# Issuing conv 2's output stores on GpSimd one group later, behind the next group's accumulating load

## The chip, the cores and the metric

The kernel runs on one core of a Trainium2 chip. The metric is the device time of one execution in microseconds (us); the median of several runs is given. The engines of the core are TensorE (PE, matrix products), VectorE (DVE), ScalarE (ACT), GpSimd (POOL) and SyncE (SP, which here only issues DMAs). Each engine takes its instructions in the order in which they stand in its queue, and waits at an instruction whose inputs aren't ready; all that stands behind it waits too.

## The reference

A residual block: group norm, SiLU and a 3x3 convolution, twice, with a time embedding added between, and the input added at the end. The input `x` is 2 images of 512 channels of 64 x 64, in bfloat16.

```python
B, C, HW, E = 2, 512, 64, 1152
def gn(z, gamma, beta):                 # 4 groups of 128 channels
    zr = z.reshape(B, G, (C // G) * H * W)
    mu = zr.mean(-1).reshape(B, G, 1)
    var = ((zr - mu) ** 2).mean(-1).reshape(B, G, 1)
    zn = ((zr - mu) / jnp.sqrt(var + eps)).reshape(B, C, H, W)
    return zn * gamma.reshape(1, C, 1, 1) + beta.reshape(1, C, 1, 1)
...
h = conv3(_silu(gn(x, g1, be1)), w1)
emb = _silu(t_emb) @ w_emb
h = h + emb.reshape(B, C, 1, 1)
h = conv3(_silu(gn(h, g2, be2)), w2)
return x + h
```

## The kernel before

Both convolutions (`layer` 0 and 1, here conv 1 and conv 2) are done by a fast scheme over rows: four output rows come from six row combinations of the activated input ("positions" 0 to 5), of which 1 and 2 (and in one chunk 3 and 4) are transformed over columns as well ("nested", tiles `nst`). The others take three column taps directly (tiles `mid` for 3 and 4, `acc` for 0 and 5).

A *chunk* is half an image, 32 rows: (b, ch) with b the image and ch the half, so there are four chunks in a convolution. For each chunk, four *groups* follow, one for each tile of 128 output channels (`ot`). A convolution thus has 16 groups, numbered 0 to 15 (`grp`). One group on TensorE is: nested products (L741), `mid` products (L730), `acc` products (L730).

The transformed input of a chunk is a tile V; V of the next chunk is made while the groups of this one run, by a background planner with due times (`bg`, `produce_V`): for each of the four input channel tiles, SP loads `src` (L420), ACT does SiLU into `ak` (L427) and a scaled copy (L433), and DVE adds and subtracts rows and columns (L442 to L491). GpSimd writes border rows with memsets (L414, L416). In conv 2, for the second chunk only, the first of the row adds (L442) is done by DMA instead: `ROWS_BY_DMA` makes GpSimd issue two accumulating DMAs from `ak` to `ak` (L437), a half each. DVE's L448 is the first instruction that needs both halves.

The scale and bias of a group norm come from `gn_scale_bias`. It has two small steps on GpSimd, L179 and L186 (`var`), between DVE steps L178 and L187. For the second image of conv 2 this is called in group 3 (`aux_plan`).

The output of a group is put together in a tile `yst` (`xr` in the last two groups) of the pool `stg`, which has three buffers. ACT copies `nst` and `mid` out (L782, L797); DVE combines rows (L804 to L813) and takes the `acc` banks in (L827). The end of group n, `close_group` and the `fin` that it returns, is carried out within group n+1, between its nested products and their evacuation (`close_prev`). For groups 0 to 13 of conv 2 (`X_BY_DMA`), `fin` adds the residual by DMA: GpSimd issues a load of `x` that accumulates into `yst` (L843), and then the store of `yst` to the output (L844), which needs the load's data. In what follows load n and store n are those of group n. For groups 14 and 15 `x` is loaded into `xr` by SP (L686) and added by DVE (L810, L815), and SP stores the output. These `xr` tiles come from the same three buffers, so the load of `xr` in group 14 waits for store 11, and that in group 15 for store 12.

The order on each engine is the order of the program, as far as the framework's scheduler keeps it; waits between engines and DMAs are placed by the framework.

Of the kernel before, what the change touches and what calls it, by code (L numbers as in the profile page):

```python
# [10 lines left out]
ALU = mybir.AluOpType  # L11
# [51 lines left out]
def kernel(  # L63
# [13 lines left out]
    nc = tc.nc  # L77
# [33 lines left out]
    x_v = x.rearrange("b (ct p) h w -> b ct p (h w)", p=P)  # L111
    out_v = out.rearrange("b (ct p) h w -> b ct p (h w)", p=P)
# [47 lines left out]
    def flat(t):  # L160
        return t[:].rearrange("p r w -> p (r w)")
# [32 lines left out]
    def after(inst, dep):  # L194
        if dep is not None:
            tc.add_manual_dep(inst.ins, dep.ins.name, SYNC_DEP, reason="dma ordering")
        return inst

    def gram_pe(pieces, grf):
# [323 lines left out]
    for i, prm in enumerate((g1, be1, g2, be2)):  # L523
        nc.scalar.dma_start(
            out=gparm[CT * i:CT * (i + 1), :],
            in_=prm.rearrange("(ct p) -> ct p", p=P),
# [70 lines left out]
    st2 = {}  # L597
    pend = []
    deferred = []

    def aux_plan(layer, g):
        acts = []
# [25 lines left out]
    for layer in range(2):  # L628
        for idx, (b, ch) in enumerate(chunks):
            for ot in range(CT):  # L630
# [49 lines left out]
                rows = slice(ch * CR * W, (ch + 1) * CR * W)  # L680
# [3 lines left out]
                if layer == 1 and not by_dma:  # L684
                    xr = stg.tile([P, CR, W], BF16, tag="io")
                    nc.sync.dma_start(  # L686
                        out=xr[:], in_=x_v[b, ot][:, rows].rearrange("p (r w) -> p r w", w=W))
# [7 lines left out]
                yst = xr if layer == 1 and not by_dma else stg.tile([P, CR, W], F16, tag="io", name="yst")  # L695
# [3 lines left out]
                last_two = grp - (len(chunks) * CT - 2) if layer == 1 else -1  # L699
# [74 lines left out]
                def scaled(o, i, f, on_act=ACT_SCALES(layer, grp)):  # L774
                    if on_act:
                        nc.scalar.activation(out=o, in_=i, func=ACT.Copy, scale=f)  # L776
                    else:
                        nc.vector.tensor_scalar(out=o, in0=i, scalar1=f, scalar2=None, op0=ALU.mult)
# [24 lines left out]
                def rows_mid(scaled=scaled, add_x=layer == 1 and not by_dma, y4=y4, sts=sts, msl=msl, tt=tt, qs=qs):  # L803
                    nc.vector.tensor_tensor(out=sts[:, 2:4], in0=msl[:, 0:2], in1=msl[:, 2:4], op=ALU.add)  # L804
                    nc.vector.tensor_tensor(out=sts[:, 0:2], in0=msl[:, 0:2], in1=msl[:, 2:4], op=ALU.subtract)
                    nc.vector.tensor_tensor(out=tt[:, 0], in0=sts[:, 2], in1=sts[:, 3], op=ALU.add)
                    scaled(qs[:, 0], sts[:, 0], 8.0)
                    nc.vector.tensor_tensor(out=tt[:, 1], in0=qs[:, 0], in1=sts[:, 1], op=ALU.add)  # L808
                    if add_x:
                        nc.vector.tensor_tensor(out=tt[:], in0=tt[:], in1=y4[:, 0:4:3], op=ALU.add)  # L810
                    scaled(qs[:, 0], sts[:, 0], 2.0)
                    scaled(qs[:, 1], sts[:, 2], 4.0)
                    nc.vector.tensor_tensor(out=qs[:] if add_x else y4[:, 1:3], in0=sts[:, 1:4:2], in1=qs[:], op=ALU.add)  # L813
                    if add_x:
                        nc.vector.tensor_tensor(out=y4[:, 1:3], in0=qs[:], in1=y4[:, 1:3], op=ALU.add)  # L815

                def close_group(layer=layer, b=b, ch=ch, ot=ot, rows=rows, yst=yst, y4=y4, tt=tt, accs=accs,
                                ssum=ssum, ssq=ssq, on_dve=on_dve, by_dma=by_dma):
                    if not on_dve:
                        for k in range(2):  # L820
                            nc.tensor.matmul(accs[(0, 5)[k]], lhsT=id_end[:, k],
                                             rhs=tt[:, k].rearrange("p t (e w) -> p t e w", e=2), start=False, stop=True)
                    for k in range(2):
                        kw = {"accum_out": ssum[:, ch, k:k + 1]} if layer == 0 else {}
                        acc = accs[(0, 5)[k]].rearrange("p t e w -> p t (e w)")
                        if on_dve:
                            nc.vector.scalar_tensor_tensor(out=y4[:, (0, 3)[k]], in0=acc, scalar=(0.25, 1.0)[k],  # L827
                                                           in1=tt[:, k], op0=ALU.mult, op1=ALU.add, **kw)
                        else:
                            nc.scalar.activation(out=y4[:, (0, 3)[k]], in_=acc, scale=(0.25, 1.0)[k],  # L830
                                                 func=ACT.Identity if layer == 0 else ACT.Copy, **kw)

                    def fin():
                      if layer == 0:
                        yf = flat(yst)
                        nc.sync.dma_start(out=h_scr[b, ot][:, rows], in_=yf)
                        junk = otmp.tile([P, CR * W], F16, tag="sts", name="junk")
                        nc.scalar.activation(out=junk[:, 0:CR * W // 2].rearrange("p (f t w) -> p f t w", f=2, w=W),  # L838
                                             in_=y4[:, 1:3], func=ACT.Identity, accum_out=ssum[:, ch, 2:3])
                        nc.scalar.activation(out=junk[:], in_=yf, func=ACT.Square,  # L840
                                             scale=float(HW) ** -0.5, accum_out=ssq[:, ch:ch + 1])
                      elif by_dma:
                        nc.gpsimd.dma_start(out=flat(yst), in_=x_v[b, ot][:, rows], accum_op=ALU.add)  # L843
                        nc.gpsimd.dma_start(out=out_v[b, ot][:, rows], in_=flat(yst))  # L844
                      else:
                        nc.sync.dma_start(out=out_v[b, ot][:, rows], in_=flat(yst))
                    return fin
# [33 lines left out]
                if first_set:  # L881
                    for pos in DIRECT + NESTED:
                        open_acc(pos)
                    aux = None
                    for ct in range(CT):
                        if ct % 2 == 0:
                            aux = ps_two.tile([P, 2, NFREE], F32, tag="two", name="aux1")
                        gn1_load(ct)
                        gn1_stats(aux[:, ct % 2], ct)
                        for pos in DIRECT + NESTED:  # L890
                            for kx in KX_ORDER:
                                mm_direct(pos, ct, kx, ct == 0 and kx == KX_ORDER[0],
                                          (pos in (1, 2, 3, 4) or on_dve) and ct == CT - 1 and kx == KX_ORDER[-1])
                    evac_mid(0)
                    evac_mid()
                    for _ in range(3):
                        bg.tick()
                    rows_mid()
                    for _ in range(3):
                        bg.tick()  # L900
                    pend.append(close_group)
                else:
                    for pos in NESTED:
                        mms(pos)
                        bg.tick()
                    if layer == 0 and grp == NFLAT - 1:
                        for f in flat_cols:
                            f()
                    if is_flat:
                        close_prev(lambda: evac_mid(0))  # L910
                    elif last_two == 1:
                        evac_nested()
                    else:
                        close_prev(evac_nested)
                    if not is_flat:
                        cols_mid()
                    mms(3)
                    bg.tick()
                    mms(4)
                    bg.tick()  # L920
                    run_aux(layer, grp)
                    if four:
                        evac_nested(1)
                        cols_mid(1)
                    else:
                        evac_mid()
                    rows_mid()
                    if last_two == 0:
                        deferred.append((end_rows, close_group))
                    elif last_two == 1:  # L930
                        ends, close = deferred.pop()
                        ends()
                        close()()
                        close_halves()
                    else:
                        for pos in (0, 5):
                            mms(pos)
                            bg.tick()
                        pend.append(close_group)
# [41 lines left out]
```

## Time and profile before

| | us |
|---|---|
| median of 3 runs | 508.08 |
| the runs | 506.97, 508.08, 510.08 |
| profiled execution | 509.58 |
| its span (first to last instruction) | 507.8 |
| TensorE busy | 486.2 (96% of the span) |
| VectorE busy | 426.1 (84%) |
| ScalarE busy | 350.9 (69%) |
| GpSimd busy | 44.1 (9%) |

The table is of one profiled execution but for its first two rows. Busy times are shares of the span and overlap each other; a wait on an engine counts only if what ends last is held up by it. Conv 2 runs from about 290 us to the end; one of its groups takes about 14 us. Loads 0 to 13 of `x` start between 299.03 and 481.69 us, and the stores between 304.94 and 487.64. A load lands 5.5 us after its issue (median), a store 3.0 us.

### The profile page before, as it was taken

How to read it: one execution, taken by the hardware profiler on the slowest of the kernel's cores; microseconds unless marked ns; L12 is line 12 of the kernel's file. 1: busy time of each engine (PE TensorE's matmuls, PEld its weight loads, DVE VectorE, ACT ScalarE, POOL GpSimd, SP SyncE). 2: the span in 40 equal slices, each digit the busy share in tenths (PEclk: the TensorE clock that was granted, in tenths of full speed). 3: DMA queues.
4: the chain of work that ended last, by engine and by line, in shares of the span. 5: the costliest groups of instructions: out<-in, count | busy, mean ns of one | idle time of the engine just before them, and what ended most of it. 6: DMA issues, size and time to landing. Idle time of an engine off the chain costs nothing. (4 is left out here: it accounts for less than half of the span.)

```text
span 507.8 us, 8116 instructions
## 1 busy us (share of the span) xinstructions
PE 486.2 (96%) x3140; PEld 285.8 (56%) x3140; DVE 426.1 (84%) x946; ACT 350.9 (69%) x341; POOL 44.1 (9%) x92
## 2 busy tenths in 40 slices
PE   4899999899999999999999999989999999999996
PEld 4865454555555555555555555545555555557784
DVE  4789899999986994469999999768998999547776
ACT  4688899699965954478999899509779633333350
POOL 1210000100000000010011002221011101110100
PEclk9679999999999999999999999989999999999999
DMA  8939231142431421133476334735554632325442
GB/s 309 365 110 333 80 119 64 45 158 92 118 95 53 142 74 43 41 121 109 152 199 178 105 87 112 155 84 130 123 134 119 124 74 55 94 71 124 122 87 83
DMA packets 24144, 61.99 MB, mean 122 GB/s; under 512 B 2219, under 2 KB 11563, under 8 KB 23723
## 3 DMA queue, kind: packets, MB, share of 16 engines
q1 hardware_dynamic: 18864, 44.64, 26.6%
q0 software_dynamic: 5184, 16.85, 15.2%
q8 instruction: 24, 0.39, 0.3%
q14 instruction: 13, 0.11, 0.1%
q10 hardware_dynamic: 59, 0.01, 0.0%
HBM read 42.54 MB, written 16.78 MB: 117 GB/s over the span
## 5 line engine op out<-in xcount | busy, mean ns | idle before, releaser
L730 PE MATMUL acc<-V,R 128*128 128x512 f16 x744 | 173.5, 390 | 3.4 <-DVE yst L827 2.6
L730 PE MATMUL mid<-V,U 128*128 128x512 f16 x720 | 167.2, 387 | 1.7 <-ACT rm L797 1.7
L730 PEld LDWEIGHTS <-R 128*128 128x128 bf16 x792 | 77.6, 99 | 95.6 <-issue 5.9
L730 PEld LDWEIGHTS <-U 128*128 128x128 f16 x720 | 70.2, 98 | 88.0 <-issue 5.3
L741 PE MATMUL nst<-V,U 128*128 128x256 f16 x1024 | 116.7, 273 | 0.0
L741 PEld LDWEIGHTS <-U 128*128 128x128 f16 x1056 | 103.3, 98 | 18.6
L782 ACT ACTIVATE rm<-nst 128x1024 f16<-128x1024 f32 x68 | 67.2, 1013 | 37.4 <-PE nst L741 24.7
L427 ACT ACTIVATE ak<-src,nb_all,sc_all 128x2112 f16<-128x2112 f16 (+1 forms) x28 | 59.9, 2143 | 9.3 <-DVE V L475 5.5
L433 ACT ACTIVATE ak<-ak 128x2112 f16<-128x2112 f16 x32 | 62.7, 1959 | 1.1 <-DVE V L473 0.4
L797 ACT ACTIVATE rm<-mid 128x1024 f16<-128x1024 f32 x30 | 30.4, 1015 | 27.3 <-PE mid L730 27.3
L776 ACT ACTIVATE qs<-sts 128x512 f16<-128x512 f16 x36 | 22.0, 626 | 28.8 <-DVE sts L804 22.9
L442 DVE TENSOR_TENSOR ak<-ak 128x2112 f16<-128x2112 f16 x28 | 34.9, 1250 | 5.7 <-ACT ak L433 5.7
L475 DVE TENSOR_TENSOR V<-ak 128x1056 f16<-128x1056 f16 x56 | 39.2, 700 | 0.3
L827 DVE SCALAR_TENSOR_TENSOR yst<-acc,tt 128x512 f16<-128x512 f32 x52 | 35.5, 683 | 1.8 <-PE acc L730 1.3
L789 DVE TENSOR_TENSOR tu<-rm 128x512 f16<-128x512 f16 x34 | 14.3, 419 | 24.8 <-ACT rm L782 24.6
L254 ACT ACTIVATE S<-R 128x1536 f16<-128x1536 bf16 (+1 forms) x28 | 31.4, 1155 | 2.7 <-DVE U L251 1.4
L838 ACT ACTIVATE junk<-yst 128x1024 f16<-128x1024 f16 x16 | 16.9, 1058 | 23.3 <-DVE yst L813 23.2
L840 ACT ACTIVATE junk<-yst 128x2048 f16<-128x2048 f16 x16 | 30.5, 1906 | 1.2 <-DVE yst L827 1.0
L251 DVE TENSOR_TENSOR U<-S 128x1536 f16<-128x1536 f16 x32 | 29.7, 948 | 0.0
L804 DVE TENSOR_TENSOR sts<-rm 128x1024 f16<-128x1024 f16 x32 | 21.9, 685 | 7.3 <-ACT rm L797 7.0
L491 DVE TENSOR_TENSOR V<-V 128x512 f16<-128x512 f16 x64 | 26.1, 431 | 0.0
L448 DVE TENSOR_TENSOR ak<-ak 128x1056 f16<-128x1056 f16 x32 | 22.5, 702 | 3.6 <-DMA ak<-ak 3.4
(124 smaller groups left out, 445.9 us busy)
## 6 DMA issues: line engine op xcount, KB each, us to landing
src<-h_scr SPq DMA_DIRECT2D x16, 528.0 KB, 4.1
h_scr<-yst SPq DMA_DIRECT2D x16, 512.0 KB, 2.7
yst<-in_x_dram POOLq DMA_DIRECT2D x14, 512.0 KB, 5.5
out_dram<-yst POOLq DMA_DIRECT2D x14, 512.0 KB, 3.0
src<-in_x_dram SPq DMA_DIRECT2D x12, 528.0 KB, 7.9
R<-in_w_dram SPq DMA_DIRECT2D x16, 384.0 KB, 4.2
xt<-in_x_dram SPq DMA_DIRECT2D x8, 512.0 KB, 5.9
g1t<-in_w_dram SPq DMA_DIRECT2D x16, 192.0 KB, 5.0
```

The costliest lines, as they stand in the source:

```text
L251: nc.vector.tensor_tensor(out=o, in0=i0, in1=i1, op=op)
L254: ts = lambda o, i, f: nc.scalar.activation(out=o, in_=i, func=ACT.Copy, scale=f)
L427: nc.scalar.activation(out=at[:, lo - r0:hi - r0, 1:W + 1], in_=sap, func=ACT.Silu, bias=nb_all[:, layer, b, ct:ct + 1], scale=sc_all[:, l ...
L433: nc.scalar.activation(out=diff, in_=same, func=ACT.Copy, scale=-4.0)
L442: nc.vector.tensor_tensor(out=diff, in0=diff, in1=below, op=ALU.add)
L475: nc.vector.tensor_tensor(out=pair(k).rearrange("p q (t w) -> p q t w", w=WP), in0=in0, in1=in1, op=op)
L730: nc.tensor.matmul(out, lhsT=w_direct(pos, ct, kx), rhs=rhs, start=first, stop=last)
L741: nc.tensor.matmul(accs["nst", (pos - 1) // 2][bank][:, q, :, plane, :], lhsT=lhsT, rhs=rhs.rearrange("p (t w) -> p t w", w=HALF), start=s ...
L782: nc.scalar.activation(out=raw[:, bank].rearrange("p q t e w -> p (q t e w)"), in_=accs["nst", k][bank][:].rearrange("p q t e w -> p (q t ...
L797: i_a = nc.scalar.activation(out=msl[:, 1 - k:4 - k:2].rearrange("p s t w -> p s (t w)"), in_=accs["mid", k][:].rearrange("p s t e w -> p ...
L827: nc.vector.scalar_tensor_tensor(out=y4[:, (0, 3)[k]], in0=acc, scalar=(0.25, 1.0)[k], in1=tt[:, k], op0=ALU.mult, op1=ALU.add, **kw)
L840: nc.scalar.activation(out=junk[:], in_=yf, func=ACT.Square, scale=float(HW) ** -0.5, accum_out=ssq[:, ch:ch + 1])
```

## The change

`fin` no longer issues the store of its own group. It issues the load, then the store that is still kept from the group before, and keeps its own. The store that is issued gets an edge to the load just issued (`behind`): it is an order for the scheduler alone and adds no wait on a semaphore. In the last two groups (`last_two >= 0`), after the row step, what is still kept is issued at once. Line numbers in the profile of before are those of the old file: L843 and L844 are the two calls with a minus.

```diff
+    ORDER_DEP = mybir.DependencyInfo(mybir.DependencyClass.NoSync, mybir.DependencyReason.SCHED_ONLY)
+
+    def behind(inst, dep):
+        if dep is not None:
+            tc.add_manual_dep(inst.ins, dep.ins.name, ORDER_DEP, reason="order")
+        return inst
...
+    to_store = []
+
+    def store_out(inst):
+        while to_store:
+            dst, y = to_store.pop()
+            behind(nc.gpsimd.dma_start(out=dst, in_=y), inst)
...
                       elif by_dma:
-                        nc.gpsimd.dma_start(out=flat(yst), in_=x_v[b, ot][:, rows], accum_op=ALU.add)
-                        nc.gpsimd.dma_start(out=out_v[b, ot][:, rows], in_=flat(yst))
+                        store_out(nc.gpsimd.dma_start(out=flat(yst), in_=x_v[b, ot][:, rows], accum_op=ALU.add))
+                        to_store.append((out_v[b, ot][:, rows], flat(yst)))
...
                     rows_mid()
+                    if last_two >= 0:
+                        store_out(None)
```

## The prediction

> **What bounds the kernel now.** I read the busy table, then the waits by total, then the order of time on GpSimd (POOL), VectorE (DVE) and TensorE (PE) from 316 to 342 us, the chain that ended last, and TensorE's clock in short stretches.
>
> ```profile
> PE 486.2 (96%) x3140; PEld 285.8 (56%) x3140; DVE 426.1 (84%) x946; ACT 350.9 (69%) x341; POOL 44.1 (9%) x92
> ```
>
> TensorE is the bound. POOL works 44 us of 508, so its own idle time costs nothing: what the change can be worth lies in what stands *behind* a waiting store on POOL's queue, if TensorE in the end waits for that. The waits (waiter, releaser, us in total, times, longest):
>
> ```profile
> POOL out_dram L844 <- DMA yst<-in_x_dram: 70.8, 14, 6.1
> DVE sc_all L187 <- POOL var L186: 6.8, 3, 4.1
> DVE ak L448 <- DMA ak<-ak: 3.4, 1, 3.4
> PE acc L730 <- DVE yst L827: 2.6, 1, 2.6
> PE mid L730 <- ACT rm L797: 1.7, 2, 1.1
> ```
>
> The first row is what the change aims at: 14 stores wait 70.8 us for their own loads. The last two rows are what TensorE loses to other engines in conv 2, 4.3 us. POOL's order of time shows what hangs on the first (start, us, instruction, idle before it and its releaser):
>
> ```profile
> 316.62 0.87 POOL L843 DMA_DIRECT2D yst<-in_x_dram  x1 [7.02 <-DVE ee L229]
> 319.61 0.87 POOL L437 DMA_DIRECT2D ak<-ak  x1 [2.12 <-ACT ak L433]
> 324.32 0.56 POOL L844 DMA_DIRECT2D out_dram<-yst  x1 [3.85 <-DMA yst<-in_x_dram]
> 324.88 0.90 POOL L437 DMA_DIRECT2D ak<-ak  x1
> ...
> 333.34 0.89 POOL L843 DMA_DIRECT2D yst<-in_x_dram  x1 [7.39 <-DVE yst L827]
> 339.15 0.56 POOL L844 DMA_DIRECT2D out_dram<-yst  x1 [4.92 <-DMA yst<-in_x_dram]
> 339.73 0.25 POOL L179 TENSOR_SCALAR var<-var 128x4 f32<-128x4 f32 x1
> ```
>
> Twice a store holds up something wanted. Store 1 (324.32) stands between the two halves of a row add by DMA (L437); store 2 (339.15) stands ahead of the group norm's `var`. Who waits for these, from the orders of time of DVE and PE:
>
> ```profile
> 328.98 0.71 DVE L448 TENSOR_TENSOR ak<-ak 128x1056 f16<-128x1056 f16 x1 [3.45 <-DMA ak<-ak]
> 331.03 0.68 DVE L827 SCALAR_TENSOR_TENSOR yst<-acc,tt 128x512 f16<-128x512 f32 x1
> 341.14 0.16 DVE L187 TENSOR_TENSOR sc_all<-var,gb 128x4 f32<-128x4 f32 x1 [4.08 <-POOL var L186]
> ...
> 331.77 7.13 PE L730 MATMUL acc<-V,R 128*128 128x512 f16 x24 [2.61 <-DVE yst L827]
> 371.43 5.50 PE L730 MATMUL mid<-V,U 128*128 128x512 f16 x24 [0.65 <-ACT rm L797]
> 386.82 5.50 PE L730 MATMUL mid<-V,U 128*128 128x512 f16 x24 [1.06 <-ACT rm L797]
> ```
>
> The first chain is whole: late second half, DVE idle 3.45 us, L827 late, TensorE idle 2.61 us. Its next 24 matmuls take 7.13 us, where the same 24 take 5.50 later on. Two short stretches say why (stretch, length, PE busy, granted clock, DMA share, GB/s):
>
> ```profile
> 328.78:332.19 3.41, 0.80 (x6) 1.00 0.00 0
> 332.19:335.60 3.41, 3.41 (x9) 0.50 0.25 22
> ```
>
> After a stretch in which TensorE worked only 0.80 us, the granted clock was half for 3.41 us: 7.13 - 5.50 = 1.6 us more. From 386.82 on TensorE has no wait left up to its last matmul at 503.8; the chain that ended last is matmuls alone there. So whatever TensorE gains up to 386.82 reaches the end whole, and nothing later can add to it.
>
> **The change part by part.** The order of instructions as built is the same on PE, DVE, ACT and SP. On POOL, store n stands right behind load n+1; stores 12 and 13 close the row. The edge adds no semaphore: store n still waits for load n, which has then landed long before (load 1 by 324.3, store 1 now behind load 2 at 333).
>
> *Second half of the row add.* Load 1, store 0, then both L437 halves, with no wait between the halves: the second goes out at 319.61 + 0.89 = 320.50 instead of 324.88, 4.4 us earlier. But it must be moved too, and store 0 now lies ahead of both halves. DMA work, as share times length, from quiet stretches: one load 3.60 x 0.92 = 3.3 us of all 16 engines (416.0 to 419.6), one store 1.60 x 0.89 = 1.4 (421.5 to 423.1), two halves 3.50 x 0.90 = 3.1 (309.0 to 312.5). From 316.50 the src load, load 1 and the first half keep the engines 0.91 busy to 323.0; then the share is 0.35 and 0.21 until 325.0, so a few engines finish some 2 us after the rest. These decide when a transfer lands. If they lag as before and take store 0 and the second half on top, the last is done at 324.8 + 1.4 + 1.5 = 327.7; DVE started about 0.5 us after the end in the DMA records (328.45 to 328.98), so L448 starts near 328.2, only 0.8 us earlier than before. Spread evenly, the work up to 325.0 (6.5 x 0.91 + 0.35 + 0.21 = 6.5) plus 1.4 and 1.5 would end at 316.5 + 9.4 = 325.9, L448 at 326.4, 2.5 us earlier. Bounds: nothing gained, and the whole 3.45. I take 0.8, since the lag is in this very row.
>
> *TensorE's wait and its clock.* The 2.61 us gap becomes 1.8. Is that enough to keep the clock? Stretches on the same grid that kept it held 2.37 us (383.39 to 386.80) and 2.10 (48.88 to 52.30) of work; one with 2.01 (18.16 to 21.58) lost it, so some 1.35 us of idle in one stretch of 3.41 is the limit. A gap of 1.8 avoids that only if a boundary parts it so that neither piece reaches 1.35, which is (2 x 1.35 - 1.8) / 3.41 = 26% of positions. So the half clock most likely stays and the 1.6 us with it; if the gap goes below 1.35 they are gained as well. [...]
>
> *`var` for the second image.* L178 ends at 337.06; L179 starts at 339.73, behind store 2. With store 1 in that place, sent off by about 334, POOL is free. What stays of DVE's 4.08 us is POOL's own work, 339.73 to 341.14 = 1.41, so 2.6 are gained. DVE and ACT are then 0.8 + 2.6 = 3.4 us ahead. TensorE doesn't wait here; what this feeds is the making of the next V, in which DVE is almost without idle from 347 to 388, and which ends in the two waits for `rm` L797, 0.65 and 1.06. With DVE and ACT 3.4 ahead and TensorE 0.8, both waits go: 1.7.
>
> *The rest* is moved at no cost I can see. Other stores have in front of them only memsets (L414, L416) nobody waits for, or the next load, which waits for DVE anyway. Each store issues 0.56 us as before. Store n releases its yst buffer one group later: store 0 goes out at 317.5, the first write to that buffer is L827 at 343.15. The nearest is SP's load of xr (L686), at 464.41 and 479.47, behind stores 11 and 12: these now leave after the loads at 469.36 and 481.69, so xr is issued near 473.5 and 486; by the 7.9 us of an x load on SP it lands at 481.5 and 494, and L810 reads it at 491.1 and 499.3. That cover is 5 us; without it, the end moves by what is missing. Behind them SP has only the last stores. Load and store now fly together, 1.4 us more DMA work beside a load; the src loads are used 5 us or more after their issue. Store 13 leaves as before, near 487.6, 16 us before the end.
>
> Sum on the profiled execution (509.58, of it span 507.8): 0.8 + 1.7 = 2.5, to 507.1. That execution lies 1.5 above the median of the runs, so I put the median at 508.08 - 2.5 = 505.6. The 2.5 is within the 3.4 that DVE and ACT allow.
>
> **Rivals.** *The gap closes below the limit.* Half lands 0.8 to 2.5 us earlier and the clock holds: TensorE could gain 0.8 + 1.6 + 1.7 = 4.1 up to 5.8, but DVE and ACT allow 0.8 + 2.6 = 3.4 up to 5.1: 504.7 down to 503.0. For it: engine work alone ends at 325.9. Against: the lagging engines.
>
> *The wait goes entirely.* 3.45 + 2.6 = 6.05 on DVE, 2.61 + 1.6 + 1.7 = 5.9 on TensorE: 502.2. Against: it wants L448's data by 325, before even the evenly spread work is done.
>
> *A transfer takes the place of the wait.* Store 0 ahead of the halves uses up all of the earlier issue: only the 1.7 of the L797 waits are left, 506.4; if these are given back too, or if the edge moves nothing that matters, 508.1.
>
> *Slower.* Store 0 pushes the halves beyond today's landing. This decides from 1.7 us later than 328.98, where it eats the L797 waits. If load 1, store 0 and the halves were served one after the other at their full median landing times (5.5 + 3.0 + 4.2 + 4.2 = 16.9 from 316.62), L448 would start at about 334, 5 us late: 5 - 1.7 = 3.3 lost, 511.4. Against: transfers one behind another overlap their fixed part in the stretches above.
>
> **How the numbers follow.** Forecast 0.50; gap closed below the limit 0.30; wait gone 0.05; transfer in its place 0.10; slower 0.05. The likeliest is 505.6. The low end of the range is the 503.0 of the first rival, the high end 508.0, where store 0 gives everything back; outside lie the wait that goes entirely and the slower case. A change within 1% (503.0 to 513.2) is about what a measurement of this kernel cannot tell from none (the runs lie 506.97 to 510.08). Faster by more: the wait gone, a part of the first rival and scatter, 0.11. Slower by more asks for over 5 us, the far end of the last rival: 0.03.
>
> **What would show it.** Right: the stores' wait on their loads is gone from the waits; the L437 halves stand 0.9 us apart; L448 still waits, 1 to 3 us; TensorE's gap there is 1 to 2.2 us; L187 waits about 1.4; the two waits for L797 are gone; PE is without idle after. Wrong: no wait of L448 at all, or one over 3.45; a new wait of DVE for a store at L827, of SP's xr at L810; a wait of `rm` for PE that shows DVE and ACT weren't ahead.

## The result, and the profile after

The changed kernel takes 504.97 us (median of 17 runs), the kernel before 508.25 in the same comparison: ratio 0.9931, 95% interval 0.9912 to 0.9949, so 3.3 us or 0.7% faster. The forecast was 505.6, in a range from 503.0 to 508.0.

In the new file the lines after the edit have moved: L448 is now L455, L827 is L840, L797 is L810, L437 is L444, the load L843 is L856, and the store is L612. I give the old numbers in words, the fences show the new ones. The busy table of the changed kernel and three of its waits (waiter, releaser, us in total, times, longest):

```profile
PE 482.8 (96%) x3140; PEld 283.9 (56%) x3140; DVE 426.2 (85%) x946; ACT 350.9 (70%) x341; POOL 44.2 (9%) x92
```

```profile
POOL out_dram L612 <- DMA yst<-in_x_dram: 4.5, 1, 4.5
DVE sc_all L187 <- POOL var L186: 4.2, 3, 1.5
DVE ak L455 <- DMA ak<-ak: 2.6, 1, 2.6
```

The stores waited 70.8 us for their loads and now wait 4.5, all of it at store 13. VectorE's longest wait for `var` fell from 4.1 to 1.5 us, its wait for the row add from 3.4 to 2.6. All engines do the same work. TensorE is busy 3.4 us less, but only 1.6 of that lies behind the gap that the change shortens, where the clock was half before. The rest lies in the first 32 us (22.9 us busy before, 21.1 now), ahead of the edit: between 10 and 20 us the granted clock was 0.66 in the one execution and 1.00 in the other. GpSimd's order of time in the changed kernel (start, us, instruction, idle before it and its releaser):

```profile
315.43 0.90 POOL L856 DMA_DIRECT2D yst<-in_x_dram  x1 [7.05 <-DVE ee L236]
315.99 0.91 POOL L612 DMA_DIRECT2D out_dram<-yst  x1
318.40 1.76 POOL L444 DMA_DIRECT2D ak<-ak  x2 [1.50 <-ACT ak L440]
...
331.29 0.90 POOL L856 DMA_DIRECT2D yst<-in_x_dram  x1 [10.97 <-DVE yst L840]
331.85 0.90 POOL L612 DMA_DIRECT2D out_dram<-yst  x1
335.11 0.23 POOL L179 TENSOR_SCALAR var<-var 128x4 f32<-128x4 f32 x1 [2.35 <-DVE var L178]
```

Store 0 follows load 1 without a wait, and both halves of the row add go out together (x2). L179 now waits for VectorE's L178 and no longer stands behind a store; what is left of VectorE's wait at L187 is GpSimd's own two steps. Who waited for these, from the orders of time of VectorE and TensorE:

```profile
326.93 0.71 DVE L455 TENSOR_TENSOR ak<-ak 128x1056 f16<-128x1056 f16 x1 [2.60 <-DMA ak<-ak]
336.50 0.16 DVE L187 TENSOR_TENSOR sc_all<-var,gb 128x4 f32<-128x4 f32 x1 [1.48 <-POOL var L186]
...
329.72 5.50 PE L743 MATMUL acc<-V,R 128*128 128x512 f16 x24 [1.73 <-DVE yst L840]
366.89 5.50 PE L743 MATMUL mid<-V,U 128*128 128x512 f16 x24
382.19 5.50 PE L743 MATMUL mid<-V,U 128*128 128x512 f16 x24 [0.96 <-ACT rm L810]
```

TensorE's gap shrank from 2.61 to 1.73 us and the 24 matmuls behind it run at full clock (5.50 instead of 7.13). The first wait for L797 (0.65) is gone; of the second, 0.96 of 1.06 is left. So TensorE gained 0.9 + 1.6 + 0.65 + 0.1 = 3.3 us. A wait for L797 costs it 0.17 us more than the idle time that the profile gives: before, `mid` started 4.72 and 4.31 us after the nested products where it waited 1.06 and 0.65, and 3.49 where it didn't wait. With one such wait less the sum is 3.4.

The profiled spans differ by more, 4.6 us (507.8 and 503.2). The rest comes from ahead of the edit: load 0 starts at 299.03 in the one and at 297.83 in the other execution, though nothing before it was changed. In the nine profiled executions of this study load 0 starts between 296.17 and 300.21; these 4.0 us are about as wide as the scatter of one kernel's runs (506.72 to 510.08 before, 502.33 to 507.67 changed). I therefore also compare the time from the start of load 0 to the end of the span: 208.8 before, 205.4 after, 3.4 us less.

### The profile page after: what moved, and what is told of

It is laid out like the page before. It is cut to its first block, busy times and chain, and to the rows that moved or that the text cites. A ratio compares the mean times of both kernels' runs of the same rounds, so it can differ in the third digit from the quotient of the medians.

```text
span 503.2 us, 8114 instructions
## 1 busy us (share of the span) xinstructions
PE 482.8 (96%) x3140; PEld 283.9 (56%) x3140; DVE 426.2 (85%) x946; ACT 350.9 (70%) x341; POOL 44.2 (9%) x92
## 5 line engine op out<-in xcount | busy, mean ns | idle before, releaser
L810 ACT ACTIVATE rm<-mid 128x1024 f16<-128x1024 f32 x30 | 30.5, 1016 | 25.9 <-PE mid L743 25.9
L840 DVE SCALAR_TENSOR_TENSOR yst<-acc,tt 128x512 f16<-128x512 f32 x52 | 35.6, 684 | 1.8 <-PE acc L743 1.3
L455 DVE TENSOR_TENSOR ak<-ak 128x1056 f16<-128x1056 f16 x32 | 22.5, 703 | 2.8 <-DMA ak<-ak 2.6
```

What stands on the lines that cost most here:

```text
L810: i_a = nc.scalar.activation(out=msl[:, 1 - k:4 - k:2].rearrange("p s t w -> p s (t w)"), in_=accs["mid", k][:].rearrange("p s t e w -> p ...
```

## The experiments

The theory: two sequences run beside each other up to the last `mid` wait at 386.82, and the later one decides. VectorE and ScalarE gain what L448 and L187 come earlier. TensorE gains what its gap shrinks, the clock behind it, and at most its two waits for L797 (1.7 us). Both depend on two stores alone: store 1 between the halves, store 2 ahead of `var`. And the halves land late because of what lies ahead of them on GpSimd's queue. All kernels keep the order of instructions on PE, DVE, ACT and SP as it was; only GpSimd's differs.

| kernel | L448 waits | L187 waits | PE gap, then 24 matmuls | waits for L797 | load 0 to end | ratio (95%) |
|---|---|---|---|---|---|---|
| before | 3.45 | 4.08 | 2.61, 7.13 | 0.65, 1.06 | 208.8 | 1 |
| changed | 2.60 | 1.48 | 1.73, 5.50 | 0.96 | -3.4 | 0.9931 (0.9912 to 0.9949) |
| only store 1 late | 1.45 | 4.18 | 0.59, 5.50 | 1.62, 0.67, 1.06 | -1.8 | 0.9943 (0.9925 to 0.9960) |
| only store 2 late | 3.57 | 1.48 | 2.71, 6.87 | none | -2.2 | 0.9958 (0.9936 to 0.9979) |
| only stores 3 to 13 late | 3.67 | 4.33 | 2.80, 8.33 | 0.99 | +0.5 | 0.9992 (0.9974 to 1.0009) |
| changed, store 0 at once | 1.50 | 1.48 | 0.67, 5.50 | 0.97 | -4.5 | 0.9892 (0.9871 to 0.9913) |
| the same, load 1 behind the halves | none | 1.48 | none, 5.50 | 0.22 | -6.0 | 0.9874 (0.9847 to 0.9902) |
| changed, store 0 twice | 3.81 | 1.48 | 2.98, 7.13 | none | -1.7 | 0.9969 (0.9946 to 0.9991) |
| changed, store 0 and half | 3.18 | 1.48 | 2.35, 7.02 | none | -2.4 | 0.9956 (0.9937 to 0.9974) |

Times are us, each from one profiled execution except for the ratio, which is of repeated runs; "load 0 to end" is the span's end less the start of load 0, as a difference to before. TensorE's own terms explain this column to 0.1 us in every row: what the gap and the 24 matmuls behind it shrink, what the waits for L797 shrink, and 0.17 us for each such wait more or less. In the second row this is 0.88 + 1.63 + 0.75 + 0.17 = 3.43.

**Only store 1 late.** The first four experiments use one condition in `fin` (`grp_` is the group): only the named groups keep their store.

```diff
                         store_out(nc.gpsimd.dma_start(out=flat(yst), in_=x_v[b, ot][:, rows], accum_op=ALU.add))
-                        to_store.append((out_v[b, ot][:, rows], flat(yst)))
+                        if grp_ in (1,):
+                            to_store.append((out_v[b, ot][:, rows], flat(yst)))
+                        else:
+                            nc.gpsimd.dma_start(out=out_v[b, ot][:, rows], in_=flat(yst))
```

> Only store 1 is issued one group later; all other stores stay right behind their own loads. Theory (two clocks, the later one decides): the two halves of the row add go out together and store 0 is not ahead of them, so DVE's L448 comes 0.85 us (as in the changed kernel) + 1.4 us (the work of store 0) = 2.2 us earlier, it still waits about 1.2, TensorE's gap shrinks from 2.6 to about 0.4 and its clock holds; but var still stands behind store 2, DVE waits there 4.1 us as before, so DVE and ACT are only 2.2 us ahead and the kernel gains 2.2 us (ratio 0.9956), with some L797 wait left on TensorE. Rival 1 (TensorE's own terms simply add): 2.2 + 1.6 of clock + 1.7 of L797 waits = 5.5 us, ratio 0.989. Rival 2 (the other stores bring the gain): 0.3 us, ratio 0.999.

Measured: ratio 0.9943; 0.9956 is inside the interval, 0.989 and 0.999 are not. The orders of time of VectorE and TensorE show why:

```profile
325.72 0.71 DVE L455 TENSOR_TENSOR ak<-ak 128x1056 f16<-128x1056 f16 x1 [1.45 <-DMA ak<-ak]
338.00 0.16 DVE L187 TENSOR_TENSOR sc_all<-var,gb 128x4 f32<-128x4 f32 x1 [4.18 <-POOL var L186]
...
328.51 5.50 PE L743 MATMUL acc<-V,R 128*128 128x512 f16 x24 [0.59 <-DVE yst L840]
353.30 5.50 PE L743 MATMUL mid<-V,U 128*128 128x512 f16 x24 [1.62 <-ACT rm L810]
368.30 5.50 PE L743 MATMUL mid<-V,U 128*128 128x512 f16 x24 [0.67 <-ACT rm L810]
383.69 5.50 PE L743 MATMUL mid<-V,U 128*128 128x512 f16 x24 [1.06 <-ACT rm L810]
```

TensorE gains 2.0 + 1.6 at the gap, more than in the changed kernel, and gives 1.6 of it back: it waits 3.35 us for L797 instead of 1.7. With `var` still late, ScalarE and VectorE are only 2 us ahead, and that is what the kernel gains. Rival 1's sum fails because it takes the waits for L797 to vanish; they grow.

**Only store 2 late.** The same condition with `(2,)`.

> Only store 2 is issued one group later. Theory: DVE's wait for var falls from 4.1 to 1.4 us, L448 still waits 3.4 us, TensorE's gap of 2.6 us and the half clock behind it stay; DVE and ACT are 2.6 us ahead but TensorE can use only its two waits for L797, 1.7 us: gain 1.7 us, ratio 0.9966, both L797 waits gone. Rival 1 (only TensorE's first gap and its clock matter): no gain, ratio 1.000. Rival 2 (what DVE and ACT gain is gained whole): 2.6 us, ratio 0.995.

Measured: ratio 0.9958. No gain at all is excluded; 1.7 and 2.6 us both lie in the interval, so the runs don't part these two. The trace does what the theory says: L187 waits 1.48, L448, the gap and the half clock stay, no wait for L797 is left.

**Only stores 3 to 13 late.** The same condition with `range(3, 14)`.

> Stores 3 to 13 are issued one group later, stores 0, 1 and 2 stay right behind their own loads. About 55 of the 70.8 us that POOL waited are removed. Theory: nobody waits for what stands behind these stores, so nothing is gained: ratio 1.000 within 0.2%. Rival (the later stores bring the gain, by freeing POOL or by moving the traffic): 2 to 3.4 us, ratio 0.993 to 0.996.

Measured: ratio 0.9992, no difference. Most of GpSimd's removed waiting is worth nothing; the change lives on two stores. In the profiled execution the half clock lasted twice as long (8.33 us for the 24 matmuls). That costs 1.2 us and the wider gap 0.2; the shorter waits for L797 give 0.9 back, which leaves the +0.5 in the table.

**Changed, store 0 at once.** The same condition with `range(1, 14)`: store 0 is no longer among the transfers ahead of the halves.

> As the changed kernel, but store 0 stays right behind its own load, so that it isn't among the transfers ahead of the two halves of the row add. Theory (the halves land late because of what is ahead of them on POOL's queue): L448 comes 0.85 + 1.4 = 2.2 us earlier than before and waits about 1.2 instead of 2.6; with var's 2.6 DVE and ACT are 4.8 ahead, TensorE could gain 2.2 + 1.6 + 1.7 = 5.5: gain 4.8 us, ratio 0.9905. Rival (store 0's place doesn't matter, load 1 and lagging DMA engines alone set the landing): L448 waits 2.6 as in the changed kernel and the gain is the same 3.4 us, ratio 0.993.

Measured: ratio 0.9892, L448 waits 1.50. Leaving store 0 where it was lets L448 come 1.1 us earlier than in the changed kernel, where the theory had 1.4, and the kernel gains 4.5 us from load 0 to the end (4.8 forecast). The rival's 2.6 us of waiting and 0.993 are out. VectorE and TensorE:

```profile
324.17 0.71 DVE L455 TENSOR_TENSOR ak<-ak 128x1056 f16<-128x1056 f16 x1 [1.50 <-DMA ak<-ak]
...
326.96 5.50 PE L743 MATMUL acc<-V,R 128*128 128x512 f16 x24 [0.67 <-DVE yst L840]
```

**The same, load 1 behind the halves.** Load 1, too, is kept until the second half of the row add has been issued.

```diff
...
-                    nc.gpsimd.dma_start(out=diff[:, part], in_=below[:, part], accum_op=ALU.add)
+                    row_adds.append(nc.gpsimd.dma_start(out=diff[:, part], in_=below[:, part], accum_op=ALU.add))
+                if len(row_adds) == 8:
+                    while row_hook:
+                        row_hook.pop()(row_adds[-1])
...
+                        elif grp_ == 1:
+                            row_hook.append(load_x)
...
```

> As e4_store0_at_once, and load 1 too is issued behind the second half of the row add, so that nothing of GpSimd's queue is ahead of the halves. Theory: the halves, issued 3 us after the place where load 1 stood, land some 4 us later, before DVE asks for them: L448 doesn't wait (1.5 in e4, 3.4 before), TensorE has no gap at acc and full clock; with var's 2.6 DVE and ACT are 6.0 ahead, TensorE's own terms are 2.6 + 1.6 + 1.7 = 5.9, so both waits for L797 go: gain 5.9 us, ratio 0.988. Rival (load 1 ahead isn't what keeps the halves: the last 1.5 us are the halves' own time): L448 waits 1.5 us and TensorE's gap is 0.6 as in e4, ratio 0.989 to 0.9905, with one L797 wait of about 1 us left.

Measured: ratio 0.9874, the fastest of all, 6 us from load 0 to the end. L448 doesn't wait, TensorE has no gap ahead of `acc`, and the last wait for L797 is 0.22. The runs alone can't part it from the kernel before it in the table (the intervals overlap); the trace does, since L448's wait is gone and not 1.5. GpSimd's order of time (in this file the halves are L445 and load 1 is L861):

```profile
319.20 1.75 POOL L445 DMA_DIRECT2D ak<-ak  x2 [10.02 <-ACT ak L441]
320.50 1.36 POOL L861 DMA_DIRECT2D yst<-in_x_dram  x1
```

**Changed, store 0 twice.** Behind store 0 the same tile is copied once more, into a scratch tile in DRAM.

```diff
...
-            behind(nc.gpsimd.dma_start(out=dst, in_=y), inst)
+            s = behind(nc.gpsimd.dma_start(out=dst, in_=y), inst)
+            if not copied:
+                copied.append(behind(nc.gpsimd.dma_start(out=more_out[:, 0:COPY], in_=y[:, 0:COPY]), s))
```

> The changed kernel with the work of store 0 doubled: right behind it, ahead of the two halves, the same tile is copied once more to a scratch buffer in DRAM. Theory (each transfer ahead of the halves delays them by its own work on the lagging engines, about 1.1 to 1.4 us for a store): L448 waits 3.7 to 4.0 us instead of 2.6, TensorE's gap is 2.8 to 3.1, so its clock falls to half again and the 24 matmuls behind it take about 7 us; TensorE's gain is then only the L797 waits less what the gap grew, 1.2 to 1.5 us, ratio 0.997 to 0.9975; L187 still waits 1.5. Rival (the ring isn't what delays the halves; a store fits into the time that load 1 needs anyway): L448 waits 2.6, gap 1.7, clock full, ratio 0.993.

Measured: ratio 0.9969, L448 waits 3.81, gap 2.98, half clock again, as the theory has it; the rival's 0.993 is out. But the second half of the row add was also issued late in this kernel and the next (after 3.90 and 3.88 us of idle time on GpSimd, last section), so the delay is not shown to be the copy's work alone.

**Changed, store 0 and half.** The same with half the size (`COPY = 1024`).

> As e6_store0_twice, but the extra copy has half the size. Theory: L448 waits 3.1 to 3.4 us and TensorE's gap is 2.2 to 2.5, between the 1.7 that kept the clock in the changed kernel and the 2.6 that lost it before. If an idle of about 2 us in one stretch of the clock's grid is the limit, the clock falls and the gain is 1.7 to 2.0 us (ratio 0.9965); if it takes more, the clock holds and TensorE and the lead of DVE and ACT allow 2.6 to 3.0 us (ratio 0.9945). Rival (no delay by the copy): as the changed kernel, ratio 0.993.

Measured: ratio 0.9956, L448 waits 3.18, gap 2.35, and the clock fell; 0.993 is out, 0.9945 is not, so it is the trace that decides on the clock. Take the four kernels that differ only in how much of store 0 lies ahead of the halves: L448 starts 10.41, 11.50, 12.08 and 12.71 us after the start of load 1 with none, one, one and a half and two stores. The first step, 1.09 us for a store, is between kernels that issue both halves together and is shown. The two steps of half a store, 0.58 and 0.63, fit it, but the late issue of the second half lies in both kernels with a copy.

The clock: in conv 2 of these traces half clock lasts 3.41 us (332.19 to 335.60 before) or twice that (328.81 to 335.63 with only stores 3 to 13 late). So the time is cut into stretches of 3.41 us, laid so that one begins where the granted clock changes (stretch, length, PE busy, granted clock, DMA share, GB/s). First the changed kernel, then the one with store 0 and half, then the one with only stores 3 to 13 late:

```profile
328.14:331.56 3.42, 1.84 (x9) 1.00 0.00 0
331.56:334.97 3.41, 3.41 (x17) 1.00 0.58 83
```

```profile
327.96:331.37 3.41, 1.27 (x8) 1.00 0.01 2
331.37:334.78 3.41, 3.20 (x8) 0.50 0.06 5
```

```profile
325.40:328.81 3.41, 1.49 (x9) 1.00 0.27 46
328.81:332.22 3.41, 2.52 (x7) 0.50 0.00 0
```

With 1.84 us of work in a stretch the next one keeps full clock, with 1.27 and with 1.49 it gets half. In the last kernel the gap reaches into the next stretch, and the one behind that, up to 335.63, runs at half clock too.

## Why the prediction was right, and where not

*What bounds the kernel, and which stores matter:* right. Two of the fourteen stores carry the whole gain.

*Second half of the row add:* right in size, 0.8 us forecast, 3.45 - 2.60 = 0.85 measured. The choice of the lagging engines over evenly spread work (2.5 us) was the right one. In the changed kernel the DMA share is 0.95 up to 325 and 0.17 in the 2 us behind that: on average 2.7 of the 16 engines, which fits a few that finish last again (the records don't name them). That the two numbers meet so closely is in part luck. Store 0's price was put at its 1.4 us of engine work; it is 1.1. And without store 0 the same terms give 0.8 + 1.4 = 2.2 us, where the kernel with store 0 at once measured 3.45 - 1.50 = 1.95. The two errors cancel.

*`var`:* right. VectorE's wait fell from 4.08 to 1.48, 2.6 as forecast. VectorE and ScalarE together came 3.4 us ahead as forecast: L187 from 341.14 to 336.50 is 4.6, less the 1.2 that the execution was ahead at load 0.

*The clock:* this is the step that failed: the limit of 1.35 us of idle, and with it the half clock and its 1.6 us that were to stay. The gap was forecast as 1.8 and came out as 1.73, but the clock held, though 1.58 us of it lay in one stretch, beyond the 1.35 that I had read as the limit. The limit came from the start of the kernel, from a stretch with 2.01 us of work that lost the clock. Of that work 0.94 us was matmuls of 128x1; whether that is why it lost the clock was not tested. In conv 2, stretches with 1.80 us of work (in the kernel with only store 1 late) and 1.84 (here) kept the clock, and those with 0.80, about 1.2, 1.27 and 1.49 lost it (before, only store 2 late, store 0 and half, only stores 3 to 13 late). So my estimate from these stretches is a limit between 1.5 and 1.8 us of work in 3.41 for these matmuls. What happened has the numbers of the first rival, 3.4 us and 504.7, and not those of the likeliest case, 2.5 and 505.6. But that rival wanted the gap below 1.35 us, and it was 1.73: the limit was wrong, and not the gap. The range held both.

*Both waits for L797 go:* wrong in consequence. With the 1.6 us of clock TensorE itself came 2.5 us ahead and met the limit of VectorE and ScalarE at 3.4; 0.96 of wait is left. The 1.7 us were also priced too low, by the 0.17 us that each wait costs beyond its idle time. It was worked out as a cap in the prediction, only not reached in its likeliest case.

*The rest moved at no cost:* right in effect, but one price was wrong. I let store 11 land 3.0 us after its issue. It now goes out right behind load 12, and stores land 6.2 us after their issue (median) instead of 3.0. The load of `xr` in group 14 went out at 472.96, in this execution some 4 us later than my steps say. L810 reads it at 486.46 and did not wait: the cover was thick enough.

*The rivals.* The wait did not go entirely here, but it does when load 1 is moved too: that kernel gained 6.0 us, and the rival's sum was 5.9. A transfer in the place of the wait was real in part: store 0 took 1.1 us of what moving store 1 gave, and with twice the store the clock is lost again. The slower case did not come: L448 came earlier, and not later.

## What to carry to other kernels

Here 70.8 us of waiting on a queue cost only what stood behind 2 of 14 waiting instructions (3.3 us; with only stores 3 to 13 moved the ratio was 0.9992): look for such instructions one by one and move just what blocks them. Moving a DMA to avoid a wait puts its bytes ahead of something else: ask what now lies ahead of the transfer that is wanted, since here leaving one store alone and moving one load more gave 6.0 us instead of 3.4 (from load 0 to the end). Where two sequences run side by side, work out the gain of each and take the smaller, before adding up a bound engine's waits.

## What was not expected of the hardware

The fifth transfer in a row on GpSimd's queue went out late in two kernels. With load 1, store 0, the copy and the first half issued within 4 us, the second half went out late, in a wait for nothing that the profile shows (kernel with store 0 twice, GpSimd's order of time; the copy is L617):

```profile
316.56 0.90 POOL L617 DMA_DIRECT2D more_out<-yst  x1
318.41 0.89 POOL L444 DMA_DIRECT2D ak<-ak  x1 [0.95 <-ACT ak L440]
323.20 0.88 POOL L444 DMA_DIRECT2D ak<-ak  x1 [3.90 <-issue]
```

In the kernel with half the copy it was 3.88 us, in the changed kernel with four transfers there was none. The late issue came 7.76 and 7.74 us after the start of load 1 in the two kernels; what it was waiting for was not tested. Whether it delayed L448 isn't shown either: in the kernel with half the copy L448 started 4.34 us after the issue of the second half, in the kernel before 4.10. The size of the copy counts all the same: with the same late issue, L448 came 0.63 us later behind the whole copy than behind half of it.

And TensorE's clock fell to half at gaps of 2.35 to 2.98 us, for 3.41 us before and for 6.82 with only stores 3 to 13 late; in the five kernels with such a gap the same 24 matmuls take 6.87 to 8.33 us instead of 5.50.
